# Products of zeros in the gap after the second burst of scores

## The chip, the cores and the metric

One core of a Trainium2 chip runs the whole kernel. The metric is the device time of one execution in microseconds; lower is better. Inputs and output are float32 in the chip's memory.

## What is computed

Attention inside chunks of 64 positions, and then a feed-forward layer on its result. With q, k and v of shape 8 x 8 x 576 x 64 (batch, heads, sequence, head dimension):

```python
scores = scale * np.matmul(q_c, k_c.transpose(0, 1, 2, 4, 3))   # chunks of 64
scores = scores - np.max(scores, axis=-1, keepdims=True)
attn = np.exp(scores)
attn = attn / (np.sum(attn, axis=-1, keepdims=True) + 1e-09)
out = np.matmul(attn, v_c)
...
x = np.ascontiguousarray(attn_out.transpose(0, 2, 1, 3)).reshape(B * S, H * D)   # 4608 x 512
a = x @ w1            # 512 x 1024
b = x @ w2            # 512 x 1024
h = a * b @ w3        # 1024 x 1024
return (h @ w_out)    # 1024 x 512
```

## The kernel before, in words

The kernel works in bfloat16 with float32 sums. It never computes h: it multiplies W3 by W_out once (`add_w3o`, for each of eight row blocks of W3: eight transposes on TensorE, L530; a copy of them out of PSUM; eight products with W_out, L541, in two parts of four; a copy of the result), and then needs three large products per tile of tokens instead of four (`add_tile`: L574 for a and b, L605 for the last).

The attention runs in groups of two chunks for all heads, 36 groups, and two groups make a burst (`add_burst`). A burst has its q and k turned (L365 for the first four groups, which are loaded as "quads", L356 or a transposing DMA later), the scores S (`s_emit`, L401), the softmax on VectorE and ScalarE (L464 maximum, L471 or L475 subtraction, L480 exponential, L484 sum, L490 division), the transposes of the weights (L495) and the product with v (`av_emit`, L412). Scores and AV products use one kind of PSUM tile, `p_at`, of two banks, and there are two such buffers that are taken in turn. All other products go through `ffn`, four buffers.

A planner decides the order of everything. Each step is added to a `Plan` with its engine, an estimated cost, a priority key, the steps that it comes after and the buffers that it takes; `plan.run()` simulates the engines with these estimates and returns the steps in order of their planned start. Each engine then executes its own steps in that order. Loads are issued by GpSimd in a fixed order (`LOADS`): the identity, the quads of q and k, pieces of W3, half of W_out, and so on; GpSimd has a limited number of loads in flight, so some of its steps wait until an earlier load has landed.

The end of the kernel holds the loop that emits the steps. Before each step of TensorE it may emit products of zeros, 128 x 128 by 128 x 512, into a PSUM tile called `warm` that nobody reads: 14 before TensorE's first step, and later one for each 0.25 us of planned idle time beyond 0.2 us, up to the first step that takes a `p_at` buffer, which is the first burst of S:

```python
zeros = consts.tile([P, TT], bf)
nc.vector.memset(zeros[:], 0.0)
warm = ps("p_at", [P, 2, TT])[:, 0]
fills, last, cold = 14, 0.0, True
```

Here `o.start` is the planned start of a step, `o.cost` its planned cost and `last` the planned end of the TensorE step before it. The tile `warm` is the first `p_at` tile; the first burst of S has the second, the second burst of S the first buffer again.

Of the kernel before, what the change touches and what calls it, by code (L numbers as in the profile page):

```python
# [177 lines left out]
def kernel(  # L178
# [27 lines left out]
    P = 128  # L206
# [3 lines left out]
    TT = 512  # L210
# [17 lines left out]
    def ps(tag, shape, dt=f32):  # L228
        return psum.tile(shape, dt, tag=tag, name=tag, bufs=BUFS[tag])
# [431 lines left out]
    with tc.manual_schedule():  # L661
        zeros = consts.tile([P, TT], bf)
        nc.vector.memset(zeros[:], 0.0)
        warm = ps("p_at", [P, 2, TT])[:, 0]
        fills, last, cold = 14, 0.0, True
        for o in plan.run():
            if o.engine == "PE":
                cold = cold and "p_at" not in o.takes
                if last:
                    fills = int((o.start - last - 0.2) / 0.25)  # L670
                for _ in range(fills if cold else 0):
                    nc.tensor.matmul(warm, zeros[:, :P], zeros[:], start=True, stop=True)
                last = o.start + o.cost
            o.emit(o.engine)


# [28 lines left out]
```

## Time and profile before

| what | value |
|---|---|
| time, three runs | 248.22, 248.40, 247.74 us (median 248.22) |
| time of the profiled execution | 249.35 us |
| its span, from the first to the last instruction | 247.6 us |
| TensorE busy | 238.8 us of the span |
| VectorE, ScalarE, GpSimd busy | 165.9, 117.0, 96.2 us |
| mean granted TensorE clock | 0.993 |

The page and the views drawn from the trace give times in microseconds from the start of the span, unless a number is marked ns. PE is TensorE's matmul side, PEld its weight loads (which overlap it), DVE is VectorE, ACT is ScalarE, POOL is GpSimd, and SP issues DMAs. "L541" is a line of the kernel. A row of the timeline has the start, the length, engine, line, operation, the tiles as output<-input, shapes, and the number of instructions merged into it; in square brackets stands the idle time of the engine ahead of it and what ended that. Products are pipelined, so the length of a row includes the drain of its last product, and the next row starts before that.

### The profile page before, as it was taken

What the parts mean: (1) busy time and instruction counts of PE and PEld (TensorE: products, weight loads), DVE (VectorE), ACT (ScalarE), POOL (GpSimd) and SP (SyncE); (2) the same over time, 40 slices, a digit from 0 to 9 for tenths busy, and PEclk for the clock granted to TensorE, in tenths of its full rate; (3) what the DMA queues carried; (4) which work ended last, traced back from release to release, by engine and by line L of the source; (5) the groups of instructions that cost most, each with busy time, mean ns of one, the idle gap of its engine ahead of it and who ended that gap; (6) DMA issues with size and microseconds to landing.
All of it is one profiled execution on the core that took longest, in us unless ns stands there. A gap on an engine that the chain in (4) does not pass through costs nothing.

```text
span 247.6 us, 5814 instructions
## 1 busy us (share of the span) xinstructions
PE 238.8 (96%) x2370; PEld 116.8 (47%) x2370; DVE 165.9 (67%) x301; ACT 117.0 (47%) x201; POOL 96.2 (39%) x119
## 2 busy tenths in 40 slices
PE   8759999999999999999999999999999999999994
PEld 2435655555544444544444444444444444444443
DVE  0368985789895887888886595967955985332310
ACT  5345774646654545534545353434543444433222
POOL 8939766886854293167224524510000000000000
PEclk9979999999999999999999999999999999999999
DMA  7999999999999999999999999999979994211114
GB/s 210 182 188 181 171 183 178 183 155 158 144 126 157 133 148 117 157 158 140 121 156 134 157 133 156 132 156 135 147 118 372 378 320 138 76 47 45 42 42 169
DMA packets 154185, 38.64 MB, mean 156 GB/s; under 512 B 141104, under 2 KB 148144, under 8 KB 154160
## 3 DMA queue, kind: packets, MB, share of 16 engines
q0 software_dynamic: 111888, 18.88, 110.5%
q1 hardware_dynamic: 41984, 18.88, 41.9%
q10 hardware_dynamic: 288, 0.52, 0.6%
q8 instruction: 18, 0.29, 0.5%
q14 instruction: 7, 0.06, 0.1%
HBM read 38.80 MB, written 9.44 MB: 195 GB/s over the span
## 4 chain that ended last, share of the span: by engine, by line
PE 91%; DMA 3%; POOL 3%; ACT 1%; issue 0%; POOLq 0%
PE ffn L574 51%; PE ffn L605 26%; PE ffn L541 6%; DMA w_sb<-in_moe_w_dram 3%; PE p_at L412 3%; PE p_at L401 2%; POOL rawq L289 2%; PE ffn L530 1%; PE ffn L356 1%; PE ffn L495 1%; ACT w3t L248 0%; POOL w_sb L313 0%; ACT w3o_sb L248 0%; POOL ident masks.py:199 0%; ACT o_sb L248 0%
## 5 line engine op out<-in xcount | busy, mean ns | idle before, releaser
L574 PE MATMUL ffn<-xt,w_sb 128*128 128x512 bf16 x576 | 132.3, 379 | 0.0
L574 PEld LDWEIGHTS <-w_sb 128*128 128x128 bf16 x576 | 54.5, 98 | 61.8
L583 DVE TENSOR_TENSOR abT<-a_sb,ffn 128x512 bf16<-128x512 f32 x72 | 49.1, 682 | 41.9 <-PE ffn L574 38.3
L605 PE MATMUL ffn<-w3o_sb,abT 128*128 128x512 bf16 (+2 forms) x304 | 67.2, 368 | 0.0
L248 ACT COPY a_sb<-ffn 128x512 f32<-128x512 f32 x72 | 42.2, 587 | 44.4 <-PE ffn L574 44.3
L270 POOL DMA_DIRECT2D raw<-in_q_dram x36 | 30.3, 844 | 35.1 <-DMA vd<-in_v_dram 13.6
L605 PEld LDWEIGHTS <-abT 128*128 128x128 bf16 x304 | 28.4, 98 | 31.1
L270 POOL DMA_DIRECT2D raw<-in_k_dram x36 | 30.3, 844 | 22.8 <-DMA vd<-in_v_dram 12.8
L464 DVE TENSOR_REDUCE nm<-p_at 128x8 f32<-128x512 f32 x36 | 23.4, 682 | 4.5 <-PE p_at L401 4.5
L248 ACT COPY o_sb<-ffn 128x512 f32<-128x512 f32 (+2 forms) x21 | 11.4, 545 | 30.6 <-PE ffn L605 30.4
L484 DVE TENSOR_REDUCE ss<-e 128x8 f32<-128x520 bf16 x36 | 24.6, 683 | 1.4 <-ACT e L480 1.4
L490 DVE TENSOR_TENSOR an<-e,rs 128x512 bf16<-128x512 bf16 x36 | 24.4, 681 | 0.2
L480 ACT ACTIVATE e<-sd 128x512 bf16<-128x512 f32 x36 | 22.1, 633 | 4.2 <-DVE sd L475 4.1
L475 DVE TENSOR_TENSOR sd<-p_at,nm 128x512 f32<-128x512 f32 x32 | 21.2, 681 | 0.0
L296 POOL DMA_DIRECT2D vd<-in_v_dram x16 | 18.5, 1166 | 3.6 <-PE ffn L574 2.6
L250 DVE CAST xt<-p_at 128x512 bf16<-128x512 f32 x18 | 12.3, 690 | 7.2 <-PE p_at L412 4.3
L541 PE MATMUL ffn<-wo_sb,w3t 128*128 128x512 bf16 x64 | 16.6, 400 | 0.3 <-ACT w3t L248 0.3
L248 ACT CAST xt<-p_at 128x512 bf16<-128x512 f32 x18 | 10.5, 587 | 7.9 <-DVE xt L250 5.5
L248 ACT COPY kqT<-ffn 128x512 bf16<-128x512 bf16 x16 | 8.9, 588 | 7.4 <-PE ffn L365 4.2
L250 DVE COPY kqT<-ffn 128x512 bf16<-128x512 bf16 x8 | 3.3, 423 | 10.1 <-ACT kqT L248 9.5
L541 PEld LDWEIGHTS <-w3t 128*128 128x128 bf16 x64 | 6.2, 103 | 6.7 <-issue 1.1
L412 PEld LDWEIGHTS <-vd 64*64 64x64 bf16 x576 | 6.0, 108 | 5.9 <-issue 5.9
(40 smaller groups left out, 128.1 us busy)
## 6 DMA issues: line engine op xcount, KB each, us to landing
out_dram<-o_sb SPq DMA_DIRECT2D x19, 256.0 KB, 2.3
vd<-in_v_dram POOLq DMA_DIRECT2D x16, 288.0 KB, 13.7
w_sb<-in_moe_w_dram POOLq DMA_DIRECT2D x16, 256.0 KB, 8.4
raw<-in_q_dram POOLq DMA_DIRECT2D x28, 128.0 KB, 10.7
raw<-in_k_dram POOLq DMA_DIRECT2D x28, 128.0 KB, 9.9
out_dram<-w_sb SPq DMA_DIRECT2D x8, 256.0 KB, 3.2
out_dram<-wo_sb SPq DMA_DIRECT2D x4, 256.0 KB, 4.5
out_dram<-rawq SPq DMA_DIRECT2D x4, 256.0 KB, 4.2
```

Of the source, the lines that this page charges most:

```text
L248: nc.scalar.copy(o, i)
L270: nc.gpsimd.dma_start(box["t"][r, w], src[b, :, c * C:(c + n) * C, :].rearrange("h p d -> p h d"))
L296: nc.gpsimd.dma_start(vds[b % len(vds)][halves[t], 2 * y0:2 * y1].rearrange("p m c d -> p (m c) d"), v[b, NM * t + 2 * y0:NM * t + 2 * y1] ...
L464: nc.vector.tensor_reduce(nm.rearrange("p (u x) o -> p u (x o)", u=2), box["sc"], axis=AX.X, op=ALU.max)
L475: nc.vector.tensor_sub(sd.rearrange("p (u x) k -> p u x k", u=2), box["sc"], box["nm"].to_broadcast([P, 8, C]).rearrange("p (u x) k -> p u ...
L480: nc.scalar.activation(e[:, :, :C], box["sd"][:], ACT.Exp, scale=scale)
L484: nc.vector.reduce_sum(ss[:], box["e"][:], axis=AX.X)
L490: nc.vector.tensor_mul(an[:], box["e"][:, :, :C], box["rs"].to_broadcast([P, 8, C]))
L541: nc.tensor.matmul(box["wp"][:], box["t"][:, ki, :], wo_sb[:, ki, :], start=(ki == wo_cut[0][0]), stop=(ki == wo_cut[-1][1] - 1))
L574: nc.tensor.matmul(t[:, :w], wt[:, ki, j * P:(j + 1) * P], x[:, ki, :], start=(ki == 0), stop=(ki == KO - 1))
L583: nc.vector.tensor_mul(box["abT"][:, j, :w], box["as", j][:, :w], box["b", j][:, :w])
L605: nc.tensor.matmul(t[:, :x1 - x0], box["abT"][:, ki, tk * P:(tk + 1) * P], w3o_sb[:, ki, x0:x1], start=(ki == 0), stop=(ki == FO - 1))
```

## The change

The loop counts how many steps have taken a `p_at` buffer (`bursts`) in place of the flag `cold`. Products of zeros may now be emitted while that count is 0 or 2: before the first burst of S, as they were, and between the second burst of S and the next step that takes a `p_at` buffer (in the planned order this is the third burst of S). For the second stretch a new `warm` tile is taken, after the second burst of S has been emitted: it lies in the buffer of the first burst of S, and so the first of its products comes after the reads of those scores. In this stretch six products are added to the number that follows from the planned gap, where this gap is over 0.1 us and the last of the step's prerequisites to end, in the plan, is a load by GpSimd.

```diff
-        warm = ps("p_at", [P, 2, TT])[:, 0]
-        fills, last, cold = 14, 0.0, True
+        warm, bursts = ps("p_at", [P, 2, TT])[:, 0], 0
+        fills, last = 14, 0.0
         for o in plan.run():
             if o.engine == "PE":
-                cold = cold and "p_at" not in o.takes
+                gap = o.start - last - 0.2
                 if last:
-                    fills = int((o.start - last - 0.2) / 0.25)
-                for _ in range(fills if cold else 0):
+                    fills = int(gap / 0.25)
+                    if bursts == 2 and gap > 0.1 and max(o.after, key=lambda d: d.end).engine == "POOL":
+                        fills += 6
+                for _ in range(fills if bursts in (0, 2) else 0):
                     nc.tensor.matmul(warm, zeros[:, :P], zeros[:], start=True, stop=True)
                 last = o.start + o.cost
             o.emit(o.engine)
+            if "p_at" in o.takes:
+                bursts += 1
+                if bursts == 2:
+                    warm = ps("p_at", [P, 2, TT])[:, 0]
```

In the built program TensorE has seven products of zeros more than before: six between the second burst of S and the transposes of the second block of W3 (L530), and one ahead of a group of four products of L541 some steps later. The order of all other instructions is the same on every engine. Line numbers after this loop's first lines shift: L672 of the kernel before is L674 of the changed one.

## The prediction

> **What bounds the kernel now.** I read the page first, then the list of waits on TensorE, then the chain of waits, then windows of time with the granted clock, and last the timeline of the stretch that the change touches. From the page, the engine totals, the granted clock in forty slices of 6.2 us (tenths of full speed) and the chain by engine:
>
> ```profile
> PE 238.8 (96%) x2370; PEld 116.8 (47%) x2370; DVE 165.9 (67%) x301; ACT 117.0 (47%) x201; POOL 96.2 (39%) x119
> PEclk9979999999999999999999999999999999999999
> PE 91%; DMA 3%; POOL 3%; ACT 1%; issue 0%; POOLq 0%
> ```
>
> TensorE is busy in 238.8 of 247.6 us and carries 91% of the chain. One slice alone stands out: the third, 12.4 to 18.6 us, with 7. All waits that end late on TensorE (total us, times, longest):
>
> ```profile
> PE ffn L530 <- DMA w_sb<-in_moe_w_dram: 2.8, 2, 2.0
> PE p_at L672 <- DVE zeros L663: 1.2, 1, 1.2
> PE ffn L365 <- DMA rawq<-in_q_dram: 1.0, 2, 0.9
> PE ffn L541 <- ACT w3t L248: 0.3, 1, 0.3
> PE ffn L365 <- DMA rawq<-in_k_dram: 0.2, 1, 0.2
> ```
>
> There is no other wait in the whole run, so after the last of these TensorE runs from instruction to instruction. The largest is 2.0 us, for a piece of W3. The chain there (start, length, what):
>
> ```profile
> 7.80 8.51 DMA w_sb<-in_moe_w_dram
> 16.36 1.04 PE ffn L530 x8
> 17.39 4.53 PE ffn L541 x16
> ...
> 21.95 0.46 ACT w3o_sb L248
> ...
> 22.46 1.02 ACT w3t L248
> 23.48 0.04 issue
> 23.52 1.04 PE ffn L541 x4
> ```
>
> The load lands at 16.31, eight transposes (L530) and sixteen products (L541) follow. Nothing but TensorE's own pace, and two ScalarE copies that follow it, lies behind that load. That pace is the point. Windows of 3.41 us (length, TensorE busy and instructions, granted clock, DMA share, GB/s):
>
> ```profile
> 9.18:12.60 3.42, 2.23 (x66) 1.00 1.23 182
> 12.60:16.01 3.41, 1.00 (x40) 1.00 1.16 191
> 16.01:19.42 3.41, 3.06 (x14) 0.50 1.75 182
> 19.42:22.83 3.41, 3.41 (x32) 1.00 1.73 172
> ```
>
> The granted clock is half for exactly one such window, 16.01 to 19.42, and the window before it had TensorE busy for 1.00 us only; a window with 2.23 us busy was followed by full clock. So the stretch with little work cost twice: the wait itself, and half speed for the work behind it. The timeline of TensorE (start, length, what, idle before):
>
> ```profile
> 13.94 0.45 PE L401 MATMUL p_at<-kqT 64*64 64x64 bf16 x32
> 16.36 1.04 PE L530 MATMUL ffn<-ident,w_sb 128*128 128x128 bf16 x8 [1.97 <-DMA w_sb<-in_moe_w_dram]
> 17.19 4.72 PE L541 MATMUL ffn<-wo_sb,w3t 128*128 128x512 bf16 x16
> 21.75 0.61 PE L530 MATMUL ffn<-ident,w_sb 128*128 128x128 bf16 x8
> 22.64 0.61 PE L356 MATMUL ffn<-ident,raw 128*128 128x128 bf16 x8
> 23.52 1.04 PE L541 MATMUL ffn<-wo_sb,w3t 128*128 128x512 bf16 x4 [0.27 <-ACT w3t L248]
> 24.40 0.61 PE L530 MATMUL ffn<-ident,w_sb 128*128 128x128 bf16 x8
> 24.84 1.03 PE L541 MATMUL ffn<-wo_sb,w3t 128*128 128x512 bf16 x4
> 25.71 0.61 PE L356 MATMUL ffn<-ident,raw 128*128 128x128 bf16 x8
> ```
>
> **The change part by part.** In the built order of instructions, TensorE gets seven more products of zeros and nothing else moves on any engine. Six stand between the second burst of S (13.94) and the transposes at 16.36; one stands ahead of the four products at 23.52.
>
> *When the six start.* Their PSUM tile lies in the banks of the first S burst, so the first of them waits for the last VectorE read of those scores:
>
> ```profile
> 13.52 1.41 DVE L471 TENSOR_TENSOR sd<-p_at,nm 128x256 f32<-128x256 f32 x4
> 14.85 0.68 DVE L464 TENSOR_REDUCE nm<-p_at 128x8 f32<-128x512 f32 x1
> ```
>
> The four subtractions end at 13.52 + 1.41 = 14.93; with 0.05 for the semaphore (the 0.04 of "issue" in the chain, rounded up) the first product starts at about 14.98. That is a new wait in TensorE's queue of 0.6 us (14.39 to 14.98); behind it stand only the six and the transposes that wait for the load until 16.31 anyway, and nobody else waits for them.
>
> *What they take.* Products of zeros are in the trace, at full clock and, at the very start, at the slow pace (there by its weight loads, one per product):
>
> ```profile
> 7.39 0.61 PE L672 MATMUL p_at<-zeros 128*128 128x512 bf16 x2
> 1.60 0.15 PEld L672 LDWEIGHTS <-zeros 128*128 128x128 bf16 x1 [0.28 <-issue]
> ```
>
> Two take 0.61 with the drain of the second, which with four products in 25.71 - 24.84 = 0.87 gives 0.218 each; at the slow pace one comes every 0.15 + 0.28 = 0.43. Six at full clock end issuing at 14.98 + 1.31 = 16.29, and the load lands at 16.31: they fit, with nothing to spare. If each took 0.43 they would end at 17.56, 1.2 us late. So the cost of the six is between 0 and 1.2 us; I take 0, since the clock is full until 16.01 in this trace.
>
> *What they bring.* The window 12.60 to 16.01 then has 1.00 + (16.01 - 14.98) = 2.03 us busy, near the 2.23 that kept the clock and far from the 1.00 that lost it. I take it that the clock stays. Then transposes and products run at the later pace: L530 to L541 24.40 to 24.84 = 0.44 in place of 17.19 - 16.36 = 0.83, saving 0.39; sixteen products at 0.218 = 3.48 in place of 21.75 - 17.19 = 4.56, saving 1.08. Together 1.47. Off this goes a wait: the second four of these products need VectorE's copy of the transposes, which now begins at 16.36 + 0.61 + 0.04 = 17.01 and by VectorE's 0.69 for such a copy ends at about 17.70, while TensorE gets there at 16.80 + 0.87 = 17.67, so 0.03, or up to 0.2 if the transposes drain as late as at half clock. The row of that copy:
>
> ```profile
> 17.43 0.69 DVE L250 COPY w3t<-ffn 128x1024 bf16<-128x1024 bf16 x1 [1.90 <-PE ffn L530]
> ```
>
> That leaves 1.27 to 1.44; I take 1.3, since the copy waits for the last drain.
>
> *The seventh product* costs 0.22 where TensorE idles 0.27 for ScalarE's copy; that copy follows the products before it, so the idle moves along and hides it. Without this cover it costs 0.22.
>
> *What is late next.* TensorE arrives 1.3 us sooner at everything behind. VectorE and ScalarE copies there wait for TensorE and move along. Loads don't: GpSimd's queue keeps its times. The rows that show landings (GpSimd steps, two of which wait for a landing; then the times to landing of three loads of W3 issued 19.94 to 21.02, and of four pieces of q and k of which that at 12.35 is the last; then the two TensorE steps furthest on):
>
> ```profile
> 12.35 0.68 POOL L270 DMA_DIRECT2D raw<-in_k_dram  x1 [0.56 <-DMA rawq<-in_q_dram]
> 18.51 0.87 POOL L270 DMA_DIRECT2D raw<-in_k_dram  x1 [1.03 <-DMA wo_sb<-in_moe_w_out_dram]
> 31.99 0.87 POOL L270 DMA_DIRECT2D raw<-in_k_dram  x1 [1.04 <-DMA vd<-in_v_dram]
> DMA to landing us min/median/max: 5.5/6.1/6.9
> DMA to landing us min/median/max: 8.9/9.8/10.2
> 27.02 0.61 PE L530 MATMUL ffn<-ident,w_sb 128*128 128x128 bf16 x8
> 33.70 0.71 PE L412 MATMUL p_at<-at,vd 64*64 64x64 bf16 x64
> ```
>
> W_out is there before 18.51; it is needed by the ninth product, 16.80 + 8 x 0.218 = 18.54. The last piece for L356 at 22.64 lands at 12.35 + 8.9 = 21.25 if the shortest time is the last piece's, needed at 21.34. The three W3 pieces land at 25.4, 26.6 and 27.9, the first is needed at 27.02 - 1.3 = 25.7, the others later. v is there before 31.99, needed by the first AV product at 33.70 - 1.3 = 32.4. All just fit, none by much; a load 0.3 later would take up to 0.3 off. I count 0, and 0.5 for the low end of the gain.
>
> **The sum.** The profiled execution took 249.35 (span 247.6, 1.75 around it); less 1.3 it is 248.05. The three runs have a median of 248.22, 1.13 below the profiled one. I carry the difference over: 248.22 - 1.3 = 246.9. That 1.13 is a weakness, though: it may be the profiler's cost, or it may be that those runs did not lose the clock.
>
> The Trainium skill (TensorE: Matmul & The Clock Gate, "Part 1: The HAM clock gate") says that the gate judges TensorE in windows of about 3.4 us that run free of the kernel's start; the 3.41 us at half clock agree. Its table "Why this matters for your kernels" allows idle gaps up to about 3 us; by that the 1.97 us gap would not cost the clock, and the fills would bring nothing, 248.2. The trace speaks against it here, for the clock fell after that gap.
>
> **The rivals.** (1) *Nothing to be had in most runs.* The half clock begins at 16.01 and lasts one window, on a grid with 12.60 and 9.18; no row ties this grid to the kernel. Moved by a microsecond, a window holds the work before 14.39 or the work after 16.36 as well, some 1.4 us, and whether that keeps the clock lies between the 1.00 and the 2.23 seen. If it does, most runs of before already have the full clock, the fills are hidden, and the time stays at 248.2, between 247.6 and 248.7. For it: the 1.13 us by which the three runs beat the profiled one is nearly the loss that I count. Against it: they spread over 0.66 us, which full clock in all doesn't explain, and profiling may cost as much.
>
> (2) *Slower: the six stand in the way.* If a window closes between 13 and 15 us with too little in it, the clock is already half when the six start; they end at 17.56 and the transposes start 1.2 us later than the load allows. It decides once a product takes more than (16.31 - 14.98) / 6 = 0.222, or if the load lands before 16.29. Price: 1.2, less what an earlier return to full clock gives back (up to 0.6): 248.8 to 249.4, say 249.1. Against it: the window to 12.60 with 2.23 busy kept the clock.
>
> (3) *The gain is eaten by loads* that just fit; a gain of 0.3 to 0.7, so 247.5 to 247.9.
>
> **How the numbers follow.** No change means within 0.3%, 0.74 us, about what a measurement of this kernel can tell. The forecast (gain of 0.75 to 1.5) has 0.56, rival 1 0.20, rival 3 0.08, rival 2 0.16. Faster 0.56, same 0.28, slower 0.16 (I count the whole of rival 2 there). The range holds the forecast, rivals 1 and 3, and leaves out most of rival 2: from 248.22 - 1.7 = 246.5 (the 1.47 and some scatter between runs) to 248.6. The forecast's own range is 246.5 to 247.5.
>
> **What would show it.** In the profile of the changed kernel: a row of six products of zeros from about 15.0, ending by 16.3 and followed by the transposes without idle; a granted clock of 1.00 from 12.60 through 22.83 if the grid lies the same; the sixteen products in 3.8 us instead of 4.72; the next transposes at 20.4 instead of 21.75; no new TensorE wait in the list; a span of 246.3. The forecast is wrong if the clock falls all the same, if the transposes start later than 16.36, or if a wait for a load of the size of the gain appears between 20 and 34 us.

## The result: slower by 0.3%

| | median of 22 runs | lowest to highest |
|---|---|---|
| before | 248.14 us | 247.38 to 248.85 |
| changed | 248.86 us | 247.89 to 249.85 |

The ratio is 1.0032, with a 95% interval of 1.002 to 1.0044. The profiled execution of the changed kernel took 249.85 us, the longest of the 22, with a span of 247.7. The forecast was 246.9 and faster; it was wrong in sign, and 248.86 lies above its range.

The timeline of TensorE in the changed kernel, the stretch that was shown of before (start, length, instructions, idle before):

```profile
13.69 0.45 PE L401 MATMUL p_at<-kqT 64*64 64x64 bf16 x32
14.88 2.38 PE L674 MATMUL p_at<-zeros 128*128 128x512 bf16 x6 [0.74 <-DVE sd L471]
17.05 1.06 PE L530 MATMUL ffn<-ident,w_sb 128*128 128x128 bf16 x8
17.91 4.01 PE L541 MATMUL ffn<-wo_sb,w3t 128*128 128x512 bf16 x16
21.75 0.61 PE L530 MATMUL ffn<-ident,w_sb 128*128 128x128 bf16 x8
23.09 0.38 PE L674 MATMUL p_at<-zeros 128*128 128x512 bf16 x1
23.53 0.82 PE L541 MATMUL ffn<-wo_sb,w3t 128*128 128x512 bf16 x3
```

The six start at 14.88, as forecast, but end late, and the transposes begin at 17.05 with no wait for their load: the row has no bracket. When that load landed is told by the GpSimd instruction that issued it (its start and length; then the time from the issue to the landing), first in the changed kernel, then, for comparison, the same time in the profile of before:

```profile
7.81 0.61 POOL L313 DMA_DIRECT2D w_sb<-in_moe_w_dram  x1
DMA to landing us min/median/max: 6.5/6.5/6.5
```

```profile
DMA to landing us min/median/max: 8.5/8.5/8.5
```

It landed at 7.81 + 6.5 = 14.3 in the changed kernel, and at 7.80 + 8.5 = 16.3 in the profile of before. The products of zeros no longer lay in a wait; they were the wait. The clock in the windows of that execution's own grid (length, TensorE busy, granted clock, DMA share, GB/s):

```profile
8.45:11.87 3.42, 2.52 (x68) 1.00 1.25 172
11.87:15.28 3.41, 1.79 (x50) 1.00 1.16 202
15.28:18.69 3.41, 3.41 (x15) 0.50 1.57 184
```

The clock fell at 15.28, while the six ran. The chain of the changed kernel shows what this did (start, length, what):

```profile
13.50 1.33 DVE sd L471 x4
14.83 0.04 issue
14.88 2.38 PE p_at L674 x6
17.26 0.85 PE ffn L530 x8
18.11 3.82 PE ffn L541 x16
```

VectorE's subtraction and then the products of zeros stand in the chain in the place of the load.

### The profile page after: what moved, and what is told of

It reads as the page before. It is cut to its first block, busy times and chain, and to the rows that moved or that the text cites. A ratio compares the mean times of both kernels' runs of the same rounds, so it can differ in the third digit from the quotient of the medians.

```text
span 247.7 us, 5828 instructions
## 1 busy us (share of the span) xinstructions
PE 240.3 (97%) x2377; PEld 117.6 (47%) x2377; DVE 165.8 (67%) x301; ACT 117.0 (47%) x201; POOL 96.3 (39%) x119
## 4 chain that ended last, share of the span: by engine, by line
PE 92%; DMA 2%; POOL 2%; DVE 1%; ACT 1%; issue 0%; POOLq 0%
PE ffn L574 51%; PE ffn L605 25%; PE ffn L541 6%; PE p_at L412 3%; PE p_at L401 2%; DMA rawq<-in_k_dram 2%; POOL rawq L289 1%; PE ffn L356 1%; PE ffn L530 1%; PE ffn L495 1%; PE p_at L674 1%; DVE sd L471 1%; DVE nm L464 0%; ACT w3t L248 0%; DVE kqT L250 0%
## 5 line engine op out<-in xcount | busy, mean ns | idle before, releaser
L541 PE MATMUL ffn<-wo_sb,w3t 128*128 128x512 bf16 x64 | 15.9, 386 | 0.1
L674 PE MATMUL p_at<-zeros 128*128 128x512 bf16 x25 | 9.1, 515 | 1.9 <-DVE zeros L663 1.2
L541 PEld LDWEIGHTS <-w3t 128*128 128x128 bf16 x64 | 6.0, 100 | 6.1 <-issue 0.5
```

What stands on the lines that cost most here:

```text
L541: nc.tensor.matmul(box["wp"][:], box["t"][:, ki, :], wo_sb[:, ki, :], start=(ki == wo_cut[0][0]), stop=(ki == wo_cut[-1][1] - 1))
```

## The experiments

Ten more runs were made, each timed beside the kernel before; two of them repeat the two kernels as they stand. An execution "lost a window" where its mean granted clock was below 0.998: 0.991 to 0.993 for one window of 3.41 us at half clock, 0.986 for two. Times are us; the fourth and fifth columns give the mean time and the number of executions of each sort. The last three are from the profile: start of the transposes (L530) that the load releases, of the next transposes (L530), and the span. Some records of products are missing from the traces, so a row can count fewer products than the kernel has.

| kernel | median | ratio to before, interval | full clock | lost a window | transposes | next | span |
|---|---|---|---|---|---|---|---|
| changed, first | 248.86 | 1.0032 (1.002 to 1.0044) | 248.24 (6) | 249.15 (16) | 17.05 | 21.75 | 247.7 |
| a_again | 249.12 | 1.003 (1.0013 to 1.0047) | 248.16 (4) | 249.28 (8) | 16.02 | 20.02 | 246.5 |
| b_again | 248.16 | 1.0 (0.9988 to 1.0012) | 248.11 (7) | 248.24 (5) | 14.54 | 19.18 | 246.0 |
| seventh | 248.21 | 1.0007 (0.9996 to 1.0019) | 248.15 (6) | 248.33 (6) | 14.56 | 20.16 | 246.4 |
| one | 248.32 | 1.0 (0.9988 to 1.0013) | 248.15 (4) | 248.25 (7) | 14.62 | 19.45 | 245.9 |
| three | 248.51 | 1.0024 (1.0008 to 1.004) | 248.37 (1) | 248.68 (11) | 16.16 | 20.33 | 246.4 |
| six_ffn | 248.79 | 1.0019 (1.0006 to 1.0032) | 248.18 (5) | 248.98 (7) | 16.71 | 20.96 | 246.8 |
| twelve | 249.95 | 1.0079 (1.0058 to 1.0101) | 249.55 (3) | 250.66 (3) | 17.75 | 21.74 | 247.6 |
| early | 248.31 | 1.0009 (0.9995 to 1.0024) | 248.38 (12) | none | 14.57 | 19.56 | 246.3 |
| swap_b | 251.24 | 1.0119 (1.0105 to 1.0133) | none | 251.26 (4) | 17.58 | 23.34 | 249.2 |
| swap_a | 249.71 | 1.0055 (1.0041 to 1.0069) | 249.68 (2) | 249.75 (3) | 17.95 | 21.96 | 247.8 |

The runs of before that were timed beside them split too: 248.09 at full clock (20) and 248.17 with a window lost (15) in the first group of four kernels; 248.09 (12) and 248.33 (17) in the second; 248.29 (4) and 248.22 (5) beside the swapped kernels. Of the 17, three lost two windows and took 248.91 to 249.12; the other 14 have a mean of 248.19.

**b_again**: the kernel before, no edit.

> The kernel before, unchanged, for its spread: which executions lose the clock. Theory A (the six products delay the load's transposes when they run at half clock): before has a dropped window about as often as the changed kernel (16 of 22 executions with a mean clock of 0.991 to 0.993), but pays less for it, spans of 245.7 to 247.6. Theory B (the six make the clock fall): before keeps 1.000 in most executions, with spans around 246.1, and shows 0.993 in few. Profile of the one look: transposes at 16.3 whatever the clock.

The time is that of before, and the profile is not like the one that the forecast was read from. The transposes follow a wait of 0.24:

```profile
13.85 0.45 PE L401 MATMUL p_at<-kqT 64*64 64x64 bf16 x32
14.54 0.62 PE L530 MATMUL ffn<-ident,w_sb 128*128 128x128 bf16 x8 [0.24 <-DMA w_sb<-in_moe_w_dram]
15.02 1.04 PE L541 MATMUL ffn<-wo_sb,w3t 128*128 128x512 bf16 x3
16.28 3.07 PE L541 MATMUL ffn<-wo_sb,w3t 128*128 128x512 bf16 x12 [0.22 <-DVE w3t L250]
19.18 0.61 PE L530 MATMUL ffn<-ident,w_sb 128*128 128x128 bf16 x8
```

And its chain runs through the loads, not through TensorE:

```profile
9.62 9.24 DMA w_sb<-in_moe_w_dram
18.86 0.28 issue
19.15 1.63 POOL w_sb L313 x3
20.78 2.28 POOL vd L296 x2
23.06 9.64 DMA w_sb<-in_moe_w_dram
```

Theory A had the transposes at 16.3 in before whatever the clock, so it fell there. Theory B had before keep the clock in most executions, and that fell too: 5 of 12 here and 15 of 35 beside it lost a window. But the loss of one window costs the kernel before only about 0.1 us (248.24 against 248.11 here, 248.17 against 248.09 beside it), because TensorE has time in hand until the loads catch it up.

**three**:

```diff
-                        fills += 6
+                        fills += 3
```

> Three products in place of the six, the one further on as before. They end at 14.9 + 3 x 0.43 = 16.2 even at half clock, before the load lands. Theory A: no delay is left, so the time is that of before or up to 0.5 better, 247.6 to 248.2, and transposes start within 0.1 of the landing. Theory B: the clock still falls as often as in the changed kernel and the time stays above before, 248.5 or more. Rival (the seventh product costs): 248.4 to 248.6.

The transposes started at 16.16, near the time that theory A gave, but the load had been there since 14.5 (issued at 7.8, 6.7 to landing), and 248.51 is above before, as B had said for another reason. Eleven of twelve executions lost a window.

**seventh**:

```diff
-                        fills += 6
+                        fills = 0
```

> Only the one product further on, none of the six. Both theories: 248.0 to 248.3, as before, since it lies in an idle time of 0.27 for a copy. If the seventh is what costs: 248.4 or more.

As expected: the single product further on costs nothing that can be measured.

**early**:

```diff
-                    if bursts == 2 and gap > 0.1 and max(o.after, key=lambda d: d.end).engine == "POOL":
-                        fills += 6
-                for _ in range(fills if bursts in (0, 2) else 0):
+                    if bursts == 1 and gap > 0.1 and max(o.after, key=lambda d: d.end).engine == "POOL":
+                        fills = 2
+                for _ in range(fills if bursts in (0, 1) else 0):
```

> No product behind the second burst of S; two each ahead of the two steps between the first and the second burst that wait for a load (idle of 0.87 each in the trace of before; two take 0.86 at half clock), in the first p_at buffer, with no new wait. They add 0.9 us of work to the windows that close between 12 and 15 us. If work in those windows decides the clock, more executions show 1.000 and the time is 247.3 to 248.0; if the clock falls for the wait up to 16.31 alone, 248.1 as before. If they delay: 248.3 or more, with the transposes of the fourth quad or of W3 later than their landing.

The products do what such products are for: none of twelve executions lost a window, against 15 of 35 of before on the same chip. The windows on that execution's own grid (the same columns as above):

```profile
8.91:12.33 3.42, 2.63 (x73) 1.00 1.28 185
12.33:15.74 3.41, 2.58 (x53) 1.00 1.15 191
15.74:19.15 3.41, 2.64 (x13) 1.00 1.72 181
```

And yet nothing is gained: 248.31, the same as before within the interval, where 247.3 to 248.0 was expected if the clock was kept. The products delay nothing either, since both transposes of W3 still wait for their loads (0.49 and 0.22). The time that a full clock saves is waited for a little later, as the waits on TensorE show (total, times, longest):

```profile
PE ffn L541 <- DMA wo_sb<-in_moe_w_out_dram: 0.8, 1, 0.8
PE ffn L356 <- DMA raw<-in_k_dram: 0.4, 1, 0.4
```

Neither wait is in the list of the profile from which the forecast was made.

**a_again**: the changed kernel, no edit.

> The changed kernel once more, for its spread on the chip of the next three and a second profile. What the first runs suggest (theory C): the load lands near 14.4 in most executions and not at 16.31, so the six stand in the way; transposes start at 16.2 to 17.1, 1.7 to 2.5 later than they could, and the loads that follow absorb about 1.7 of it. Then 248.6 to 249.0, executions at full clock near 248.2, those that lose a window near 249.1.

As expected by theory C, at 249.12 a little above its range. The profile fell on an execution at full clock:

```profile
14.71 1.47 PE L674 MATMUL p_at<-zeros 128*128 128x512 bf16 x5 [0.53 <-DVE sd L471]
16.02 0.61 PE L530 MATMUL ffn<-ident,w_sb 128*128 128x128 bf16 x8
16.46 3.71 PE L541 MATMUL ffn<-wo_sb,w3t 128*128 128x512 bf16 x16
20.02 0.61 PE L530 MATMUL ffn<-ident,w_sb 128*128 128x128 bf16 x8
21.25 0.61 PE L356 MATMUL ffn<-ident,raw 128*128 128x128 bf16 x8 [0.17 <-DMA raw<-in_k_dram]
```

(One record of the six is missing.) The transposes are 1.5 late against before's 14.54, but TensorE still waits for k at 21.25: the lateness is absorbed. At half clock it is not, and the 24 executions of the changed kernel that lost a window stand 0.9 to 1.1 above the 10 that didn't.

**one**:

```diff
-                        fills += 6
+                        fills += 1
```

> One product of zeros in place of the six: the wait for the scores' reads stays, five products go. Theory C (how long the queue is held decides): the transposes start at 14.9 + 0.2 to 0.4 = 15.1 to 15.3, 0.7 late, which the loads that follow absorb: 248.1 to 248.4. Theory D (the wait for the reads and the clock that falls in it decide): as with the six, 248.6 or more.

Theory C: 248.32, ratio 1.0. The wait for the scores' reads is still there (idle 0.54 ahead of the one product), and costs nothing by itself; 7 of 11 executions lost a window and stand only 0.1 above the others. Theory D fell.

**twelve**:

```diff
-                        fills += 6
+                        fills += 12
```

> Twelve in place of six. Theory C: the slack is used up by the six, so the further six come on top, 1.3 at full clock and up to 2.6 at half: 249.9 to 251.0. If the products lie beside a wait that is there anyway, as the forecast had it: under 249.3. If more work keeps the clock and the clock is what counts: below the 248.9 of the six.

Theory C: 249.95. At full clock the further six cost 249.55 - 248.16 = 1.4 (their bare length is 6 x 0.22 = 1.3), where the first six cost 0.1 at most.

**six_ffn**: the six in a buffer that needs no wait, the seventh product left out.

```diff
-                for _ in range(fills if bursts in (0, 2) else 0):
+                for _ in range(fills if bursts == 0 or bursts == 2 and fills > 5 else 0):
...
-                    warm = ps("p_at", [P, 2, TT])[:, 0]
+                    warm = ps("ffn", [P, TT])
```

> Six products as in the change, in a buffer of the other kind of PSUM tile (ffn) that is free, so without the wait for the scores' reads; the seventh left out. They start at 14.1 and end at 15.5 at full clock, 16.7 at half. Theory C: transposes 1.0 late at full clock, absorbed: 248.1 to 248.5, with less lost than in the change, and near 249 only where the clock is half. Theory D: no wait, the clock holds in nearly all executions, 248.2 or less.

The median, 248.79, is above the range that theory C gave and nearly that of the change, since 7 of 12 executions lost a window; those at full clock are at 248.18 and the others at 248.98, as C said of each sort. Where the six begin matters less than that they run at half clock in the way. Theory D had the clock hold without the wait, and fell here too.

**swap_b and swap_a**: the kernel before and the changed one, with two loads in the other order (half of W_out ahead of the second piece of W3).

```diff
-            o.emit(o.engine)
+            if o is not w3_got[1]:
+                o.emit(o.engine)
+            if o is wo_got[1][0]:
+                w3_got[1].emit("POOL")
```

> The kernel before with two loads issued in the other order: W_out's half ahead of the second piece of W3, so that this piece lands near 17.9 instead of 14.4, as a lasting copy of the late landing on which the forecast was built (16.31). All theories: transposes at 17.9, an idle time of 3.5 ahead of them, the clock lost in most executions, and the next transposes at 21.9 at full clock or up to 23.3 at half, so 249.5 to 251.

> The changed kernel with the same two loads swapped. The six now lie beside a wait that is there anyway: 14.9 to 16.2 at full clock, to 17.5 at half. If the forecast's mechanism holds where the load is late: no delay of the transposes, the clock kept or regained before the sixteen products, and 0.5 to 1.5 less than the swapped kernel before. If the products of zeros bring nothing even there: within 0.3 of it. If they delay: more than it.

Here the forecast's gain appears. First the swapped kernel before, then the swapped changed kernel, TensorE's timeline:

```profile
17.58 1.04 PE L530 MATMUL ffn<-ident,w_sb 128*128 128x128 bf16 x8 [3.43 <-DMA w_sb<-in_moe_w_dram]
19.27 4.24 PE L541 MATMUL ffn<-wo_sb,w3t 128*128 128x512 bf16 x14 [0.22 <-issue]
23.34 0.61 PE L530 MATMUL ffn<-ident,w_sb 128*128 128x128 bf16 x8
```

```profile
14.69 0.61 PE L674 MATMUL p_at<-zeros 128*128 128x512 bf16 x1 [0.43 <-DVE sd L471]
15.52 1.91 PE L674 MATMUL p_at<-zeros 128*128 128x512 bf16 x4 [0.22 <-issue]
17.95 0.62 PE L530 MATMUL ffn<-ident,w_sb 128*128 128x128 bf16 x8 [0.52 <-DMA w_sb<-in_moe_w_dram]
18.41 3.71 PE L541 MATMUL ffn<-wo_sb,w3t 128*128 128x512 bf16 x16
21.96 0.61 PE L530 MATMUL ffn<-ident,w_sb 128*128 128x128 bf16 x8
```

The load is late for good, the six end ahead of it even at half clock, TensorE has the full clock again when it lands, and the next transposes come 23.34 - 21.96 = 1.4 sooner. The windows ahead of the load, in the same order, show how:

```profile
11.16:14.57 3.41, 1.62 (x56) 1.00 1.13 181
14.57:17.98 3.41, 0.40 (x4) 0.50 1.28 196
```

```profile
11.06:14.47 3.41, 1.62 (x56) 1.00 1.12 191
14.47:17.88 3.41, 2.52 (x5) 0.50 1.22 199
```

The clock falls in both after a window with 1.62 us of work. With 0.40 us in the next window it stays at half, and the transposes and most of the products run slow; with the six in it, 2.52 us, it is full from 17.88. In this execution, then, the six do not keep the clock, as they were to do in the forecast; they win it back while TensorE waits. (In two of the five the clock never fell, and one of the four without the six lost a single window and took 251.35; these have no trace.) The times: 251.24 (4 runs, 251.22 to 251.35) and 249.71 (5 runs, 249.47 to 249.95), 1.5 less. Both stay above the kernel before, since a late load costs more than this.

## Why the prediction was wrong, point by point

**The step that failed is the landing at 16.31.** It was taken from the one profiled execution as the load's time, and it was that execution's alone. In all nine later profiles with this order of loads it landed 6.3 to 6.8 us after its issue, at 14.1 to 14.6. The prediction had a sign of it and named it a weakness: the profiled execution was 1.13 us above the median of the runs. The span says the same, 247.6 against 246.0 in b_again. The profiler's cost, which the prediction allowed for, is not the reason: the profiled execution of b_again took 248.00, no more than its median of 248.16. None of the 107 other executions of before reached 249.35; the longest took 249.12. Carrying the gain over to the median counted a loss that most runs don't have.

**The bound went with it.** That "TensorE runs from instruction to instruction" behind the wait was true of that execution, in which TensorE was late enough to meet every load. In an ordinary one the loads of weights carry the chain to 28 us and further. The table shows the bend: as long as the next transposes start by about 20.3 the span is 245.9 to 246.5, and from there it follows them one to one (20.96 gives 246.8, 21.75 gives 247.7, 23.34 gives 249.2). "All just fit, none by much" was the right sign read the wrong way: loads that just fit when TensorE is 1.3 us sooner are loads for which it waits when it is 2 us sooner, as it usually is (19.18 in b_again against 21.75).

**What the six cost** was bounded by 0 and 1.2, and 0 was taken. At full clock this is right (0.1), but by luck: the transposes are still 1.5 late, and a later wait hides it. Where the clock falls they take 2.38 instead of 1.31, the transposes and products behind run slow as well, and the sum is 0.9 to 1.1. Two executions of three lost a window, so the median lies there.

**What the six bring** was counted as 1.47, less a wait. The loss of one window costs the kernel before about 0.1; early, which keeps the clock, gains nothing. Of the 1.47 nothing is to be had where the load is in time; with the load late, 1.5 was measured. The three executions of before that lost two windows stand 0.9 above those at full clock, but none of them has a trace.

**The window.** 2.03 us of work were to keep the clock. The window that closed at 15.28 had 1.79 and lost it. The prediction used the grid of one execution; in the profiles the half clock begins at 16.01, 15.28, 14.91, 13.81 and 13.11, and lasts 3.41 each time. The Trainium skill (TensorE: Matmul & The Clock Gate, "Part 1: The HAM clock gate") states that the window is free-running and doesn't reset when the kernel starts; these starts agree. The limit of about 3 us of idle in that page's table "Why this matters for your kernels", which the prediction set against the trace, does not hold here: the longest idle stretch ahead of the loss at 15.28 is below 1 us.

**The rivals.** Rival 2 is what happened, at the price that it gave (248.8 to 249.4; measured 248.86 and 249.12), and by a condition that it named, "if the load lands before 16.29"; it had 0.16, since that condition was taken for the exception. Rival 1 was right on before: its ordinary time holds no loss to win back. Its reason was another, though: not that the clock is kept, but that losing one window is nearly free. The seventh product costs nothing, as forecast.

Two things stay open. Why the load was 2 us late in the one execution is not known. And with six products ahead of the transposes a window was lost in 24 of 34 executions, against 37 of the 73 of before that ran beside the experiments; that the idle ahead of the first product (0.74) is the reason is not shown. With a like idle (0.54) and one product it was 7 of 11 (one), with the six but without the wait 7 of 12 (six_ffn), with three products 11 of 12, and such counts don't separate the reasons.

## What to carry to other kernels

A profile is one execution: where it lies above the runs, find the event that makes it longer before costing an edit against that event, and ask whether a second execution has it. Filling a wait with dummy work is safe only where the wait is sure, because the filling stands in the queue when the awaited thing comes early; here it helps by 1.5 us with a load that is always late and costs 0.7 to 1.0 with one that is usually early. And a slow stretch is worth nothing as long as what follows it waits for loads: look for the next wait behind it in an ordinary execution, not in the one in which the slow stretch has hidden it.

## What was not expected of the hardware

The clock falls after a window that is half full, not only after an idle one. Windows on each execution's own grid, with the TensorE time in them: 0.40, 1.00, 1.62, 1.77, 1.78, 1.79 and once 1.98 of 3.41 us were followed by half clock; 1.89, 2.09 and more by full clock. Where the clock never fell, the grid is counted in steps of 3.41 from the point at which the opening products of zeros go over from the slow pace to the full one (in a_again behind the weight load at 5.01). Here are two such windows, each with the one behind it, from the profiles of seventh and a_again (the second column is the busy time; the clock stands in the window after it):

```profile
11.50:14.91 3.41, 1.78 (x56) 1.00 1.15 200
14.91:18.32 3.41, 3.19 (x12) 0.50 1.50 189
```

```profile
11.95:15.36 3.41, 1.89 (x50) 1.00 1.11 179
15.36:18.77 3.41, 3.41 (x23) 1.00 1.54 185
```

The limit thus lies near 1.8 to 2.0 us, with some overlap, as ends of products in the trace are modelled and records can be missing.
